# Moving SyncE's first load ahead of the preset of its bounds registers

## The chip, the cores and the metric

One core of one Trainium2 chip. The metric is the device time of one execution in microseconds (us); lower is better. Most executions of one kernel agree here within 0.4 us, that is 0.1%. Kernels are compared only within the same rounds.

## The reference, cut to what matters

One decode step of a small model: a gated mix of a grouped-query attention over a long cache and a gated MLP.

```python
# x: (1, 1, 1024); k_cache, v_cache: (1, 4, 65536, 128), all bf16
g = _sigmoid((x * gate_w).sum(-1, keepdims=True))
a = _A_ref(x, A_k_cache, A_v_cache, A_wq, A_wo)   # softmax(q k^T) v, then @ wo
b = _B_ref(x, B_w_in, B_w_sp, B_b_sp, B_w_out)    # gelu, layernorm, gating, @ w_out
return g * a + (1 - g) * b
```

With one query row almost nothing is reused: each weight and each cache row is read once. 162 MB have to come from HBM (the page of before: 162.01 MB read).

## The kernel before

All large loads go through one helper, on SyncE's DMA queue. The helper notes the name of the very first one. When the program is finished, a callback takes that load out of its written place, behind the entry barrier, and puts it into the entry block, ahead of SyncE's drain. The barrier is: every engine drains and reports; GpSimd waits for four reports, then releases all. (In the records of before the last of the five drains ends at 0.557 us, GpSimd's two semaphore instructions start at 0.583 and 0.661 us, and those of the other four engines at 0.703 to 0.715 us.)

```python
    first_load = []

    def start_first_load(n):
        blocks = n.main_func.blocks
        # ... finds the load named in first_load: block, i, ins
        assert not ins.has_wait()
        del block.instructions[i]
        head = blocks[0].instructions
        at = next(i for i, x in enumerate(head)
                  if x.engine == ins.engine and type(x).__name__ == "InstDrain")
        head.insert(at, ins)

    nc.at_finalize(start_first_load)
    # ...
    def load(src, shape, at):
        # ... v is a slice of the one large buffer kv
        ins = nc.sync.dma_start(out=v, in_=src)
        if not first_load:
            first_load.append(ins.ins.name)
        return v
    # ... the first calls: two halves of w_in, two of wq, then the keys
    win_t = [load(win_view[:, i * KH:(i + 1) * KH, :], (KH, F), 3 + i) for i in range(2)]
    wq_t = [load(wq_view[:, i * KH:(i + 1) * KH, :], (KH, HD), 1 - i) for i in range(2)]
```

The entry block lists for SyncE (the other engines have the same head, without the load; GpSimd has one more instruction, INC_SWDGE_SEM, ahead of its four presets, and four memsets behind them). The bounds registers are the four that the listing calls bcreg; "bounds" is the reading of that name:

```
RegisterMove  SP_zero = 0
TPBBaseLd     SP_tpb_base_lo, SP_tpb_base_hi
RegisterMove  SP_bcreg0_lo = 0xffffffff      # the four bounds registers
RegisterMove  SP_bcreg0_hi = 0xffffffff
RegisterMove  SP_bcreg1_lo = 0xffffffff
RegisterMove  SP_bcreg1_hi = 0xffffffff
DMACopy       kv <- in_B_w_in_dram           # the first load, before the change
Drain, EventSemaphore                        # the entry barrier
```

Of the kernel before, what the change touches and what calls it, by code (L numbers as in the profile page):

```python
# [28 lines left out]
def kernel(  # L29
# [70 lines left out]
    def start_first_load(n):  # L100
        blocks = n.main_func.blocks
        found = None
        for block in blocks:
            for i, ins in enumerate(block.instructions):
                if ins.name in first_load:
                    found = (block, i, ins)
        block, i, ins = found
        assert not ins.has_wait()
        del block.instructions[i]
        head = blocks[0].instructions  # L110
        at = next(i for i, x in enumerate(head)
                  if x.engine == ins.engine and type(x).__name__ == "InstDrain")
        head.insert(at, ins)

    nc.at_finalize(start_first_load)

    out_queues = []
# [404 lines left out]
    for i, queue in enumerate((nc.scalar, nc.sync)):  # L522
        p0 = (2 * i + 1) * B - 1
        ins = queue.dma_start(out=out_rows[2 * i:2 * i + 2, :], in_=out_sb[p0:p0 + 2, :])
# [40 lines left out]
```

## Time and profile before

PE is TensorE, DVE is VectorE, ACT is ScalarE, POOL is GpSimd and SP is SyncE.

| | before |
|---|---|
| median of 3 runs | 383.24 us (383.21 to 383.49) |
| span of the profiled run | 381.4 us |
| moved by SyncE's queue | 162.01 MB, from 1.01 to 380.59 us: 426.8 GB/s |
| PE, DVE busy | 61%, 57% of the span |

Part 2 of the page of before cuts the span into 40 equal slices; a digit is the busy share in tenths, and the last row is the rate in GB/s.

```profile
PE   0433467678157944796397629872967196849355
DVE  4241487996687506966977059669780488550040
DMA  9999999999999999999999999999999999999995
GB/s 376 439 426 416 433 436 440 436 461 429 400 426 440 440 435 426 440 440 440 440 428 440 440 440 433 428 427 406 433 440 428 426 433 427 440 411 436 440 405 230
```

Neither PE nor DVE stays at 9 for more than two slices in a row; the DMA engines are at 9, that is 90% or more, until the last slice. Read packet by packet, fewer than 15 packets of this queue are in flight for only 0.02 us in all between 3 and 375 us. The kernel is one uninterrupted stream of loads.

Part 4 of the same page follows the chain of work that ended last, as shares of the span:

```profile
DMA 59%; PE 20%; DVE 16%; issue 2%; ACT 1%; SPq 1%; DVEq 0%; ACTq 0%
```

More than half of that chain is waiting for loads. The rest is compute that ran while the queue still had loads in hand, as the slices show.

The timeline of before at its start (columns: start in us, duration, engine, line, operation, output <- input, count; SPq and ACTq are the DMA issues of SyncE and ScalarE; other lines are cut, here and below):

```profile
0.00 1.11 SPq L167 DMA_DIRECT2D kv<-in_B_w_in_dram  x2
0.23 0.10 POOL L549 MEMSET const-float32-0.0<- 128x1 f32 x1 [0.23 <-issue]
0.79 0.58 ACTq L181 DMA_DIRECT2D xg<-in_A_x_dram  x1
1.16 0.97 SPq L167 DMA_DIRECT2D kv<-in_A_wq_dram  x2
```

The first load's issue is the very first record and so the zero point of the span. The second load, the other half of w_in, is merged into the same line; it is issued at 0.785 us, behind the barrier.

The timeline merges rows and leaves control instructions out. The trace's single records have them. SyncE's first records in before, in nanoseconds:

```
start   took  operation
    0    382  DMA_DIRECT2D      first load
  436    121  DRAIN             entry barrier, report
  703     17  EVENT_SEMAPHORE   entry barrier, release
  785    328  DMA_DIRECT2D      second load
```

### The profile page before, as it was taken

What the parts mean: (1) busy time and instruction counts of PE and PEld (TensorE: products, weight loads), DVE (VectorE), ACT (ScalarE), POOL (GpSimd) and SP (SyncE); (2) the same over time, 40 slices, a digit from 0 to 9 for tenths busy, and PEclk for the clock granted to TensorE, in tenths of its full rate; (3) what the DMA queues carried; (4) which work ended last, traced back from release to release, by engine and by line L of the source; (5) the groups of instructions that cost most, each with busy time, mean ns of one, the idle gap of its engine ahead of it and who ended that gap; (6) DMA issues with size and microseconds to landing.
All of it is one profiled execution on the core that took longest, in us unless ns stands there. A gap on an engine that the chain in (4) does not pass through costs nothing.

```text
span 381.4 us, 2581 instructions
## 1 busy us (share of the span) xinstructions
PE 232.4 (61%) x1372; PEld 56.8 (15%) x796; DVE 218.4 (57%) x211; ACT 39.6 (10%) x55; POOL 4.4 (1%) x10
## 2 busy tenths in 40 slices
PE   0433467678157944796397629872967196849355
PEld 0110011112011210121011101120111011212123
DVE  4241487996687506966977059669780488550040
ACT  1010001111601100114010001050001010500000
POOL 4000000000000000000000000000000000000000
PEclk9966659998759895989588959895799679969766
DMA  9999999999999999999999999999999999999995
GB/s 376 439 426 416 433 436 440 436 461 429 400 426 440 440 435 426 440 440 440 440 428 440 440 440 433 428 427 406 433 440 428 426 433 427 440 411 436 440 405 230
DMA packets 4375, 162.17 MB, mean 425 GB/s; under 512 B 520, under 2 KB 524, under 8 KB 908
## 3 DMA queue, kind: packets, MB, share of 16 engines
q1 hardware_dynamic: 4324, 162.01, 98.7%
q8 instruction: 8, 0.13, 0.1%
q14 instruction: 3, 0.02, 0.0%
q10 hardware_dynamic: 40, 0.01, 0.0%
HBM read 162.01 MB, written 0.00 MB: 425 GB/s over the span
## 4 chain that ended last, share of the span: by engine, by line
DMA 59%; PE 20%; DVE 16%; issue 2%; ACT 1%; SPq 1%; DVEq 0%; ACTq 0%
DMA kv<-in_A_k_cache_dram 37%; PE s_ps L391 15%; DVE kv L384 9%; DMA kv<-in_A_wo_dram 8%; DMA kv<-in_A_wq_dram 7%; DMA kv<-in_A_v_cache_dram 7%; PE o_ps L437 3%; DVE pt L427 2%; DVE mx L386 1%; DVE o_sb L451 1%; PE q_ps L277 1%; ACT sc L424 1%; DVE rowt L447 1%; ACT sc L402 1%; SPq L167 1%
## 5 line engine op out<-in xcount | busy, mean ns | idle before, releaser
L391 PE MATMUL s_ps<-kv,wt 128*128 128x512 bf16 x512 | 142.1, 437 | 81.8 <-DVE kv L384 81.7
L384 DVE STREAM_TRANSPOSE kv<-kv 128x2048 int32<-128x2048 int32 x64 | 142.7, 2280 | 55.5 <-DMA kv<-in_A_k_cache_dram 55.5
L437 PE MATMUL o_ps<-kv,pt 128*64 128x512 bf16 x512 | 61.6, 399 | 7.7 <-DMA kv<-in_A_v_cache_dram 7.7
L391 PEld LDWEIGHTS <-wt 128*128 128x128 bf16 x256 | 27.5, 108 | 197.6 <-issue 140.2
L402 ACT CAST sc<-s_ps 128x1024 bf16<-128x1024 f32 x16 | 16.2, 1013 | 253.5 <-PE s_ps L391 253.5
L437 PEld LDWEIGHTS <-pt 128*64 128x64 bf16 x256 | 16.0, 115 | 50.7 <-issue 48.1
L427 DVE STREAM_TRANSPOSE pt<-sc 128x1024 bf16<-128x1024 bf16 x16 | 18.6, 1217 | 6.8 <-ACT sc L424 6.8
L386 DVE TENSOR_REDUCE mx<-sc 128x1 f32<-128x1024 bf16 x12 | 14.5, 1207 | 10.1 <-ACT sc L402 10.1
L424 ACT ACTIVATE sc<-sc,nb 128x1024 bf16<-128x1024 bf16 x16 | 18.2, 1137 | 12.2 <-DVE nb L420 12.2
L447 DVE TENSOR_TENSOR rowt<-o_ps,own 128x1024 f32<-128x1024 f32 x4 | 4.8, 1194 | 24.9 <-PE o_ps L437 24.9
L457 PE MATMUL om_ps<-o_sb,hsel 128*32 128x128 f32 x8 | 2.5, 421 | 19.7 <-DVE o_sb L451 19.7
L406 DVE TENSOR_REDUCE mx<-sc 128x1 f32<-128x1024 bf16 x4 | 4.9, 1220 | 14.2 <-ACT sc L402 14.2
L277 PE MATMUL q_ps<-kv,xT 128*32 128x512 bf16 x64 | 7.2, 627 | 7.4 <-DMA kv<-in_A_wq_dram 7.4
L478 PE MATMUL out_ps<-kv,oa 128*32 128x256 bf16 x128 | 6.7, 366 | 3.7 <-DMA kv<-in_A_wo_dram 2.2
L277 PE MATMUL z_ps<-kv,xT 128*32 128x448 bf16 x64 | 6.2, 570 | 3.8 <-DMA kv<-in_B_w_in_dram 3.8
L344 DVE TENSOR_TENSOR rowt<-q_ps,own_b 128x512 f32<-128x512 f32 x2 | 1.3, 686 | 12.5 <-PE q_ps L277 12.5
L451 DVE TENSOR_REDUCE o_sb<-rowt 128x128 f32<-128x1024 f32 x4 | 7.5, 1872 | 0.1
L292 DVE TENSOR_TENSOR rowt<-z_ps,own_b 128x448 f32<-128x448 f32 x2 | 1.2, 620 | 8.5 <-PE z_ps L277 8.5
L233 PE MATMUL xb_ps<-xg,spread 8*128 8x256 bf16 x1 | 0.4, 367 | 9.1 <-DMA xg<-in_gate_w_dram 9.1
L277 PEld LDWEIGHTS <-xT 128*32 128x32 bf16 x64 | 3.0, 139 | 19.4 <-issue 19.3
L478 PEld LDWEIGHTS <-oa 128*32 128x32 bf16 x128 | 4.4, 124 | 6.1 <-issue 3.3
L521 ACT CAST out_sb<-out_ps 128x256 bf16<-128x256 f32 x1 | 0.4, 372 | 45.4 <-PE out_ps L478 45.4
(88 smaller groups left out, 54.8 us busy)
## 6 DMA issues: line engine op xcount, KB each, us to landing
kv<-in_A_k_cache_dram SPq DMA_DIRECT2D x4, 4096.0 KB, 26.8
kv<-in_A_wq_dram SPq DMA_DIRECT2D x2, 4096.0 KB, 32.8
kv<-in_A_v_cache_dram SPq DMA_DIRECT2D x2, 4096.0 KB
kv<-in_B_w_in_dram SPq DMA_DIRECT2D x2, 3584.0 KB, 15.0
kv<-in_A_wo_dram SPq DMA_DIRECT2D x1, 4096.0 KB
kv<-in_B_w_out_dram SPq DMA_DIRECT2D x1, 3584.0 KB
kv<-in_A_wo_dram SPq DMA_DIRECT2D x1, 2048.0 KB, 28.6
kv<-in_A_wo_dram SPq DMA_DIRECT2D x1, 1024.0 KB, 30.7
```

The source lines that it names most:

```text
L277: ins = nc.tensor.matmul(ps[t * B:(t + 1) * B, k * HN:k * HN + n], lhsT=xT[:, i * KH + c:i * KH + c + 1].to_broadcast([P, B]), rhs=w[:, c, ...
L384: nc.vector.transpose(out=kb[:, v * n:(v + 1) * n], in_=kb[:, v * n:(v + 1) * n])
L386: nc.vector.reduce_max(**late.pop())
L391: ins = nc.tensor.matmul(s_ps[:, k * HN:(k + 1) * HN], lhsT=wt[g % 2][:, v, b].rearrange("p a v h -> p (a v h)"), rhs=kx[:, b // 2, b % 2, ...
L402: nc.scalar.copy(out=sct[g, j][:], in_=s_ps[:])
L406: nc.vector.reduce_max(**late.pop())
L424: nc.scalar.activation(out=sct[g, j][:], in_=sct[g, j][:], func=ACT.Exp, scale=SCALE, bias=nb[:, 0:1], accum_out=lss[g][:, j:j + 1])
L427: nc.vector.transpose(out=ptt[g, j][:].rearrange("p c x -> p (c x)"), in_=sct[g, j][:])
L437: ins = nc.tensor.matmul(o_ps[g][hs, e, :], lhsT=ptt[g, j][:, 2 * u:2 * u + 2, :].rearrange("p c x -> p (c x)"), rhs=vx[:, 2 * u + e], sta ...
L447: nc.vector.tensor_tensor(out=om8, in0=o_ps[g][:].rearrange("p e (v d) -> p (e v) d", d=DH), in1=own_8[:].unsqueeze(2).to_broadcast([P, 2 ...
L451: nc.vector.tensor_reduce(out=o_sb[:], in_=om8.rearrange("p x d -> p d x"), axis=AX.X, op=ALU.add)
L478: nc.tensor.matmul(out_ps[t * B:(t + 1) * B, :], lhsT=vec[:, c0 + c:c0 + c + 1].to_broadcast([P, B]), rhs=w[:, c, t * NO:(t + 1) * NO], st ...
```

## The change

The intent is to start the stream earlier still. The load doesn't need the barrier: in before it is issued at 0, the barrier's release stands at 0.703 us. That it doesn't need the bounds registers either was the author's assumption (experiment 1, with every preset deleted, gave a correct result). So it is put directly behind the load of the base address, ahead of the four presets.

```diff
         head = blocks[0].instructions
         at = next(i for i, x in enumerate(head)
-                  if x.engine == ins.engine and type(x).__name__ == "InstDrain")
-        head.insert(at, ins)
+                  if x.engine == ins.engine and type(x).__name__ == "InstTPBBaseLd")
+        head.insert(at + 1, ins)
```

## The prediction

> **What bounds the kernel.** The load stream. In the 40 slices the DMA row is 9 in all but the last; PE is busy 61% and DVE 57% of the span (first part of the page). Read packet by packet, SyncE's queue moves 162.01 MB from 1.01 us after the span's start to 380.59 us: 426.8 GB/s, with 15 or more packets in flight but for about 0.5 us at the head and 4 us at the tail. The chain of waits agrees: its head is a 28.19 us load, its tail a 31.88 us load of wo, three matmuls, a cast and the store. So whatever moves the first byte by X should move the last by X.
>
> **What the change does.** Nothing is added or removed. In the entry block SyncE runs: zero register, load of the base address, four register moves (bounds), first load, drain. Afterwards the load stands ahead of the four moves.
>
> **Its cost.** The moves are not recorded. GpSimd has the same four between two records: its first instruction ends at 0.158 us and its first memset starts at 0.232 us, so four take at most 74 ns. [...] X is about 70 ns; less, if the base address is still being loaded and the moves now hide behind it.
>
> **What it can't touch.** The entry barrier closes on SyncE: its drain runs from 0.436 to 0.557 us and arrives last; GpSimd releases at 0.66 us and the second load issues at 0.785 us. SyncE executes the same instructions ahead of its drain either way, so the barrier, the second load, ACT's loads and all compute keep their absolute times. The second load is issued long before the first (3.67 MB, about 8.6 us at 427 GB/s) has drained, so the stream has no hole and carries the 70 ns to the end. The first matmuls (9.13 us, z at 12.66 us) may shift by a packet (about 1.07 us), but wq lands only at 29.35 us: slack.
>
> **Prediction.** 383.24 − 0.07 = **383.17 us, range 382.7 to 383.7**. The three runs of before spread by 0.28 us, four times the gain: most of the range is noise. Faster by over 2% 0.005, within 2% 0.99, slower 0.005.
>
> **What the profile would show.** The span starts with the load's issue, the trace's first record, so its zero point moves: it should stay at 381.4 us (381.0 to 381.8) even if the time falls. Counted from the first issue, everything behind the barrier should appear 0.07 us *later*: the first memset at about 0.30 us, the second load at 0.85, ACT's first load at 0.86, SyncE's drain 0.12 us behind the end of the load's issue instead of 0.054. The first packet should still come 1.01 us behind the issue. If those gaps stay as they were, X is zero.
>
> **What would make it wrong.** The load may have to wait for the base address: X is 0. The timed interval may start with the first load, which hides X. The load may delay SyncE's drain and the barrier by some 0.1 us, which costs nothing. Another interleaving of packets may change the mean rate: 0.1% is 0.38 us, of either sign.

X, about 70 ns, stands on GpSimd's gap of at most 74 ns alone. The 18 ns for one move in the expectations below are about a quarter of that gap. That the base address might still be loading was a possibility; no trace shows such a load.

## The result, and the profile after

The changed kernel took 383.37 us (median of 6 runs, 383.12 to 383.48), before 383.23 us (6 runs, 383.12 to 383.49). The ratio is 1.0002, 95% interval 0.9989 to 1.0014: the same. Ratios here and below are those for the fast runs of the same rounds; they are not quite the ratio of the medians quoted.

Part 2 and part 4 of the page of after:

```profile
PE   0433466678147934796389538762977196849355
DVE  4241487996689406966986059668860497550040
DMA  9999999999999999999999999999999999999995
GB/s 370 438 416 429 436 435 436 440 461 402 421 440 433 440 428 433 440 440 440 433 435 440 440 440 426 428 420 419 440 426 442 426 419 441 440 400 440 436 408 230
```

```profile
DMA 67%; PE 17%; DVE 12%; issue 2%; ACT 1%; SPq 1%; DVEq 0%; ACTq 0%
```

The stream is the same (426.7 GB/s, before 426.8). The chain's shares differ (DMA 67% for 59%) though the time does not, and the two programs will turn out to be one. Such a shift is no evidence of a change. (Probably a load and a compute step end close together at some places, and the chain follows now one, now the other; no run tests this.)

The timeline of after at its start:

```profile
0.00 1.13 SPq L167 DMA_DIRECT2D kv<-in_B_w_in_dram  x2
0.23 0.10 POOL L549 MEMSET const-float32-0.0<- 128x1 f32 x1 [0.23 <-issue]
0.81 0.59 ACTq L181 DMA_DIRECT2D xg<-in_A_x_dram  x1
1.18 0.95 SPq L167 DMA_DIRECT2D kv<-in_A_wq_dram  x2
```

The prediction named its own test: GpSimd's first memset should now appear 0.30 us behind the load's issue, because the load had moved and the memset had not. It stands at 0.23 us, as before. SyncE's drain should come 0.12 us behind the end of the issue; it comes at 451 ns behind an issue of 397 ns, the same gap of 54 ns as before. By that test X, the prediction's name for the gain, is zero; the test does not say why. SyncE's first records in after:

```
start   took  operation          after (in ns)
    0    397  DMA_DIRECT2D      first load
  451    126  DRAIN
  722     17  EVENT_SEMAPHORE
  805    328  DMA_DIRECT2D      second load
```

What stands behind the barrier comes 0.02 us later than in the trace of before, as the issue took 15 ns longer; experiment 7 shows that this does not come from the change.

The compiled programs say why. Building both kernels and comparing what the compiler hands to each engine gives five pairs of files that are equal byte for byte. SyncE's stream opens in both with a call and a block label, which every engine has, then come the DMA, the drain and the semaphore wait. There is no register move and no load of a base address in it, on any engine: nothing in the program reads those registers, and they had been dropped after the callback. "Ahead of the presets" and "behind the presets" are the same place. The presets are already missing from the program that the build hands to the compiler: the end of the build drops them, not the compiler. The reason, that nothing reads the registers, was tested by a build too: the kernel of experiment 2 below, without the one line that names its four registers as read, loses its four moves and gives the files of before.

### The profile page after: what moved, and what is told of

The parts are those of the page before. It is cut to its first block, busy times and chain, and to the rows that moved or that the text cites. A ratio compares the mean times of both kernels' runs of the same rounds, so it can differ in the third digit from the quotient of the medians.

```text
span 381.5 us, 2581 instructions
## 1 busy us (share of the span) xinstructions
PE 229.3 (60%) x1372; PEld 56.7 (15%) x796; DVE 218.4 (57%) x211; ACT 39.6 (10%) x55; POOL 4.4 (1%) x10
## 4 chain that ended last, share of the span: by engine, by line
DMA 67%; PE 17%; DVE 12%; issue 2%; ACT 1%; SPq 1%; DVEq 0%; ACTq 0%
DMA kv<-in_A_k_cache_dram 45%; PE s_ps L391 13%; DVE kv L384 9%; DMA kv<-in_A_wo_dram 8%; DMA kv<-in_A_wq_dram 7%; DMA kv<-in_A_v_cache_dram 7%; PE o_ps L437 3%; DVE mx L386 1%; DVE pt L427 1%; PE q_ps L277 1%; SPq L167 1%; DVE o_sb L451 0%; ACT sc L424 0%; DVE rowt L447 0%; ACT sc L402 0%
## 5 line engine op out<-in xcount | busy, mean ns | idle before, releaser
L391 PE MATMUL s_ps<-kv,wt 128*128 128x512 bf16 x512 | 137.8, 425 | 85.9 <-DVE kv L384 85.8
L437 PE MATMUL o_ps<-kv,pt 128*64 128x512 bf16 x512 | 62.7, 404 | 7.4 <-DMA kv<-in_A_v_cache_dram 7.4
L402 ACT CAST sc<-s_ps 128x1024 bf16<-128x1024 f32 x16 | 16.2, 1012 | 253.3 <-PE s_ps L391 253.3
```

Of the source, the lines that this page charges most:

```text
L391: ins = nc.tensor.matmul(s_ps[:, k * HN:(k + 1) * HN], lhsT=wt[g % 2][:, v, b].rearrange("p a v h -> p (a v h)"), rhs=kx[:, b // 2, b % 2, ...
L402: nc.scalar.copy(out=sct[g, j][:], in_=s_ps[:])
L437: ins = nc.tensor.matmul(o_ps[g][hs, e, :], lhsT=ptt[g, j][:, 2 * u:2 * u + 2, :].rearrange("p c x -> p (c x)"), rhs=vx[:, 2 * u + e], sta ...
```

## The experiments

**Theory A:** the presets are not in the compiled program, so before and after are one program. **Rival B:** the presets run, but the load gains nothing because they ran hidden beside the load of the base address. **Rival C:** the load did move by about 70 ns, and the noise hides it. Beside these, the prediction's estimate of what four moves cost, and its claim that a shift of the first byte arrives whole at the last byte, had to be tested by themselves, since the change tested neither.

Every variant was built from the kernel before. For the table at the end, times inside a trace are counted from GpSimd's first memset, whose program is the same in all variants; the zero of the span is of no use, because it moves with the first record.

### 1. No presets at all

```diff
         head.insert(at, ins)
+        for i in reversed(range(len(head))):
+            if type(head[i]).__name__ in ("InstRegisterMove", "InstTPBBaseLd"):
+                del head[i]
```

> All twenty bounds presets, the zero registers and the loads of the base address are deleted from the entry block of every engine; the load stands where it stood before the change. Theory A (the presets are removed as dead before the compiled program, so before, after and this are one program): the trace's entry is as in before to within 0.02 us - GpSimd's first memset 0.23 us behind the load's issue, GpSimd's gap of 0.074 us between its first instruction and its first memset still there although no move is left, SyncE's drain 0.054 us behind the issue's end; time within 0.2 us of before. Rival B (the presets run, hidden behind the base address's load): GpSimd's gap of 0.074 us shrinks to about 0.01 us. Rival C (they run and cost 70 ns, but the noise hid it): the first memset appears at 0.23 us or less only because both engines lose the same four moves, the gap on GpSimd shrinks too.

Measured: 383.22 us (5 runs, 383.16 to 383.40), before 383.18 us in the same rounds, ratio 1.0001 (0.9988 to 1.0013). Its compiled streams equal those of before too, so this run is before against itself once more. The outputs are right. The first memset stands at 0.232 us and SyncE's drain at 441 ns, 59 ns behind the end of the issue. On GpSimd, where the prediction had read the cost of four moves from a gap, the gap is unchanged with no move left:

```
start   took  operation          GpSimd, no presets (before: the same, last line 232, 99)
  131     27  INC_SWDGE_SEM
  232     98  MEMSET
```

So those 74 ns were never four moves. Theory A holds, B and C fall with their own expectation that the gap shrinks.

### 2. Four moves that the compiler must keep, ahead of the load

Four registers are set, and named as read at the end of the program, so that the moves stay. The callback puts the moves directly ahead of the first load.

```diff
+    for i in range(4):
+        live_regs.append(nc.sync.alloc_register(f"live{i}"))
+        live_moves.append(nc.sync.reg_mov(live_regs[i], i + 1).ins.name)
     win_view = B_w_in.rearrange("(p c) n -> p c n", c=KC)
     ...
         head.insert(at, ins)
+        # cut: a loop moves the instructions named in live_moves to head[at]
     ...
+    nc.sync.keepalive_nop([nc.sync.lower_val_access(r) for r in live_regs])
```

The compiled SyncE stream has four more instructions than before, and the other four engines' streams are unchanged.

> Four register moves that the compiler must keep (their registers are read at the end) stand ahead of the first load on SyncE. Theory A: now the moves are in the program and the load comes about 4 x 18 = 0.07 us later than the other engines' first records: GpSimd's first memset about 0.16 us behind the load's issue instead of 0.23, DVE's drain at about 0.05 instead of 0.12. Time +0.07 us, which the spread of 0.3 us hides: within 0.2 us of before. Rival B (moves hide behind other work of SyncE): the memset stays at 0.23 us. If a move costs more than the prediction's estimate, the shift divided by four says how much.

Measured: 383.43 us (5 runs, 383.39 to 383.53), before 383.18 us, ratio 1.0006 (0.9993 to 1.0018). The interval includes 1, but no run lies below 383.39, and only one of the nine of before lies above it (383.48). SyncE's first records (the barrier's release is cut, here and in experiment 3):

```
start   took  operation          four kept moves ahead
    0     40  MOVE
   70     34  MOVE
  128     29  MOVE
  179     29  MOVE
  249    391  DMA_DIRECT2D       first load
  692    118  DRAIN
 1038    328  DMA_DIRECT2D       second load
```

```profile
0.24 0.10 POOL L561 MEMSET const-float32-0.0<- 128x1 f32 x1 [0.24 <-issue]
0.25 1.12 SPq L175 DMA_DIRECT2D kv<-in_B_w_in_dram  x2
```

This timeline of the variant has the order of before reversed: the memset comes first, the load 0.005 us after it. Two things follow. The trace does record register moves, so their absence from the records of before and after meant absence from the program, not blindness of the profiler. And the expectation was wrong in size: it had the load 0.07 us late, but it is 0.237 us late (0.232 + 0.005). The moves start 70, 58 and 51 ns apart and the load 70 ns behind the last; the estimate of 18 ns each was less than a third of that.

### 3. The same four moves behind the load

This is the change as it was meant, on a program in which the moves exist.

```diff
         head.insert(at, ins)
+        at += 1
+        # cut: the same loop
```

> The change as it was meant, on a program in which the four moves exist: they stand behind the load instead of ahead of it. The moves of the earlier runs started 52 ns apart, so: load's issue back to 0.23 us ahead of GpSimd's first memset, SyncE's drain some 0.21 us further behind the issue's end (about 0.27 us instead of 0.054), second load at about 1.0 us instead of 0.785; time as before, about 0.25 us below the kernel with the moves ahead. If the moves' place didn't matter, the two would have the same time.

> The kernel with four kept moves ahead of the load once more, now in the same rounds as its counterpart with the moves behind: 0.2 to 0.3 us above before and above that counterpart, with the first packet 0.24 us later against GpSimd's first memset.

Measured in the same rounds: behind 383.23 us (5 runs, 383.19 to 383.29), ahead 383.43 us (5 runs, 383.29 to 383.64), before 383.24 us (9 runs). Ratios to before 1.0000 (0.9988 to 1.0013) and 1.0006 (0.9993 to 1.0018). The medians are 0.20 us apart and the runs of the two kernels meet only at 383.29. One program against itself gave a difference of medians of up to 0.15 us (experiment 7), so the clock alone would be thin evidence; but experiment 2 gave the same on another chip, and in the trace the first packet comes 0.24 us earlier with the moves behind. So, where the moves are real, their place is worth about 0.2 us, in the direction that the change intended. The timeline and the records with the moves behind:

```profile
0.00 1.24 SPq L175 DMA_DIRECT2D kv<-in_B_w_in_dram  x2
0.23 0.10 POOL L561 MEMSET const-float32-0.0<- 128x1 f32 x1 [0.23 <-issue]
```

```
start   took  operation          four kept moves behind
    0    387  DMA_DIRECT2D       first load
  431     40  MOVE
  501     34  MOVE
  559     29  MOVE
  610     29  MOVE
  679      7  DRAIN
  908    327  DMA_DIRECT2D       second load
```

The second load is 0.12 us later than in before (908 against 785 ns), not the expected 0.21: the drain took 7 ns here, against 121 ns where it stands directly behind the issue of a DMA. That lateness cost nothing that the times show (383.23 us, before 383.24 us).

### 4. Forty-eight moves ahead of the load

The edit is that of 2 with `range(48)`.

> The same with 48 such moves, a dose large enough for the clock. At 18 ns each the first load is issued 48 x 18 = 0.86 us later. If the first byte's shift is carried to the last byte and the timed interval starts ahead of the load, as the prediction had it, the time rises by 0.86 us (0.5 to 1.2), to about 384.1 us, ratio about 1.002. If the timed interval starts with the load, the time stays within 0.2 us. In the trace the memsets now come before the load, and the entry barrier about 0.86 us later.

Measured: 385.76 us (5 runs, 385.54 to 385.94), before 383.18 us, ratio 1.0066 (1.0053 to 1.0079). The timeline:

```profile
0.24 0.10 POOL L561 MEMSET const-float32-0.0<- 128x1 f32 x1 [0.24 <-issue]
2.54 1.13 SPq L175 DMA_DIRECT2D kv<-in_B_w_in_dram  x2
3.33 0.60 ACTq L189 DMA_DIRECT2D xg<-in_A_x_dram  x1
```

The rise of 2.58 us is three times the 0.86 us expected, again because of the size of a move: 48 of them put the issue at 2.535 us, 53 ns each. What the run was for came out clearly. Counted from the first memset, the first packet is 2.52 us later than in before, the last landing 2.50 us later, and the time 2.58 us longer. The shift passes through whole, and the timed interval does begin ahead of the load.

### 5. Forty-eight moves behind the load

> The 48 moves stand behind the first load and ahead of SyncE's drain. First load as in before, the barrier and the second load about 0.86 us later (second load at about 1.65 us instead of 0.785). The first load's 3.67 MB keep the rings busy for about 8.6 us, so theory: time within 0.2 us of before, although the barrier, all engines' starts and the x loads are 0.86 us late. If the start of the compute mattered, the time would rise by up to 0.86 us.

Measured: 383.28 us (5 runs, 383.23 to 383.35), before 383.18 us, ratio 1.0001 (0.9987 to 1.0015). From its timeline:

```profile
0.00 0.41 SPq L175 DMA_DIRECT2D kv<-in_B_w_in_dram  x1
0.23 0.10 POOL L561 MEMSET const-float32-0.0<- 128x1 f32 x1 [0.23 <-issue]
3.24 0.33 SPq L175 DMA_DIRECT2D kv<-in_B_w_in_dram  x1
3.24 0.59 ACTq L189 DMA_DIRECT2D xg<-in_A_x_dram  x1
```

The second load and every engine's start are 2.46 us late (3.241 against 0.785 us; the expected 1.65 used the same 18 ns), and the time stays within the spread. The first load alone keeps the queue fed for about 8.6 us (3.67 MB at 427 GB/s, an estimate from the size and the measured rate). The barrier is off the path (2.46 us late, no cost that shows); the issue of the first load is on it (first packet 2.52 us late, 2.58 us longer, experiment 4).

### 6. No early start

The line `nc.at_finalize(start_first_load)` is removed; the load stands in its written place behind the barrier.

> The load stands in its written place, behind the entry barrier, with no early start at all. In before it is issued at 0 and the second load at 0.785 us; without an issue of 0.38 us ahead of SyncE's drain the barrier closes about 0.15 us or more earlier, on the next slowest engine, so the first load should come some 0.4 us behind its place in before, and the time rises by that amount, 0.3 to 0.8 us (about 383.7). If the time stayed, the head of the stream would not be on the path, against the run with 48 moves ahead.

Measured: 383.88 us (5 runs, 383.82 to 384.04), before 383.24 us, ratio 1.0018 (1.0005 to 1.0030).

```profile
0.24 0.10 POOL L548 MEMSET const-float32-0.0<- 128x1 f32 x1 [0.24 <-issue]
0.73 0.86 SPq L166 DMA_DIRECT2D kv<-in_B_w_in_dram  x2
```

The load comes 0.50 us behind the memset instead of 0.23 us ahead of it, 0.73 us later in all. The expected 0.4 us was too low: without a load ahead of it the barrier released SyncE only 0.055 us earlier, counted from the memset (652 − 236 ns against 703 − 232), because by the records GpSimd's own drain was then the last to end, 252 ns behind the memset (488 − 236), where in before SyncE's had been, 325 ns behind it. The time rose by 0.64 us. The early start that before already had is therefore worth 0.64 us, and it was the whole of what could be had by placing this load: in the compiled stream nothing but the opening call and label stands ahead of the load.

### 7. The changed kernel again, and four looks at the entry

> The changed kernel once more, timed in more rounds. Its compiled instruction streams are byte for byte those of before, so this is before against itself: ratio 1.000, medians within 0.2 us, and the records at the entry within 0.02 us of those of before. A rival that lets the change act on the chip needs the load's issue at 0.25 us or more ahead of the first memset.

Measured: 383.09 us (5 runs, 383.00 to 383.38), before 383.24 us, ratio 0.9999 (0.9985 to 1.0012). One program against itself gave a difference of medians of +0.14 us the first time and of −0.15 us now. That is the noise of the comparison.

In the records of this run the first load's issue took 397 ns once more, against 382 ns in before and in experiment 1. It was the only difference between the traces that seemed to sort by the placing, so four looks were taken, two of each placing, two of them with comment lines on top:

> The kernel before, unchanged, for one more look at the entry. In two profiles each so far the first load's issue took 382 ns in the placing of before and 397 ns in the changed one, though the instruction streams are byte for byte the same. If that 15 ns is chance of a loaded program, this look and the three beside it give a mix of values between 380 and 415 ns that does not sort by the placing; if it belongs to the placing, this one gives 382 ns again.

> The changed kernel, unchanged, one more look. 397 ns again if the 15 ns belongs to the placing; anything between 380 and 415 ns if it is chance. GpSimd's first memset 0.23 us behind the load's issue either way, and no recorded register move.

> The kernel before with two comment lines at its top: the same instructions, other line numbers. 382 ns if the 15 ns belongs to the placing; 380 to 415 ns if chance.

> The changed kernel with two comment lines at its top: the same instructions, other line numbers. 397 ns if the 15 ns belongs to the placing; 380 to 415 ns if chance.

Measured: the issue took 398 ns in before, 397 ns in before with comment lines, 398 ns in after and 398 ns in after with comment lines. All four have the larger value; it does not belong to the placing. They were run on another chip. The variants of experiments 2 to 6 took 387 to 412 ns. What sets it stays open; it is 15 ns. The single times were 383.24, 383.19, 383.36 and 383.14 us, beside 383.12 us for before (one run each, state unknown), and say no more.

### All timed runs together

Columns 2 and 3 are differences to the one kept trace of before, whatever chip each trace is from, each counted from GpSimd's first memset, for the packets of SyncE's queue; the last landing is that of the output's store. Column 4 is the difference of the medians of the same rounds. All in us.

| kernel | first packet | last landing | time |
|---|---|---|---|
| after (first rounds) | +0.01 | +0.08 | +0.14 |
| 1 no presets | −0.01 | +0.03 | +0.04 |
| 2 four moves ahead | +0.23 | +0.22 | +0.25 |
| 3 four moves ahead, again | +0.24 | +0.38 | +0.19 |
| 3 four moves behind | +0.01 | +0.03 | −0.01 |
| 4 forty-eight ahead | +2.52 | +2.50 | +2.58 |
| 5 forty-eight behind | +0.01 | +0.10 | +0.10 |
| 6 no early start | +0.74 | +0.56 | +0.64 |
| 7 after, again | +0.02 | −0.17 | −0.15 |

The last landing scatters by up to 0.19 us around the first packet's shift: the mean rate of the 380 us stream differs a little from run to run (from first packet to last landing 426.81 GB/s in before, 426.74 GB/s in after). The time follows the first packet within that scatter.

## Why the prediction was right or wrong

The forecast of the time held: 383.37 us measured for 383.17 predicted, inside 382.7 to 383.7, and "within 2%" was right. But its reason for a gain was wrong. That the number held was luck: the forecast gain was a quarter of the noise, and the range was so wide with noise that it would have held anything from a loss of 0.4 us to a gain of 0.5 us.

- **"What bounds the kernel": right.** 48 moves moved the first packet by 2.52 us, the last landing by 2.50 us and the time by 2.58 us. What moves the first byte moves the last.
- **"X is about 70 ns": the step that failed.** X is 0. The prediction took the list of the entry block at the callback for what SyncE runs. The four moves and the base address's load are dropped afterwards, in the build, since nothing reads them; before and after are the same program. The prediction had allowed X = 0, but for another reason, a wait for the base address; there is no base address load to wait for.
- **"GpSimd has the same four between two records": wrong.** The gap of 74 ns has no instruction in it in the compiled stream, and stays when the presets are deleted (experiment 1). That a move takes 18 ns was thus an estimate that no record showed. Real moves on SyncE start about 52 ns apart (mean of the 48 in experiment 4).
- **"The moves are not recorded": true of before, but for the wrong reason.** The trace records moves where there are any (experiments 2 to 5). An instruction missing from the records should have raised the question whether it exists.
- **"The barrier ... keep[s its] absolute times": true of this pair only because nothing moved.** In the program that has the moves, putting them behind the load closed the barrier 0.12 us earlier than with the moves ahead (second load at 676 against 794 ns after the memset), since the drain shortened from 118 to 7 ns. In before the other engines' drains of this barrier took 10 ns on VectorE, 8 ns on ScalarE and on TensorE, and 186 ns on GpSimd, behind its first memsets. The barrier's place has no effect on the time that these runs show: with 2.46 us of lateness it was 383.28 us, before 383.18 us (experiment 5).
- **"The first packet should still come 1.01 us behind the issue": right.** It was 1.01 us in before and 1.02 us in after. Counted from the end of the issue it is 0.63 us in before (1012 − 382 ns).
- **"If those gaps stay as they were, X is zero": right**, and it was the quickest way to the answer: a test of 70 ns that the clock, with a spread of 0.3 us, could not make.

## What to carry to other kernels

Before costing an instruction that a diff moves past another, make sure that both are in the compiled program: compare the compiled streams of the two kernels, since a list taken inside the build may still hold code that is dropped as dead. In this kernel, one unbroken stream of loads, what stood ahead of the first issue on the issuing engine counted about one for one (2.52 us of first packet for 2.58 us of time), and the barrier behind that issue could come 2.46 us late without a measurable cost. For effects far below the spread of the times, read the gap between the records of two engines, one of which the change does not touch, and use a large dose to calibrate the clock.
